# Block-causal attention followed by a bilinear FFN on one core: weight conversions of the first pass emitted step by step, at 0.8 parts a slot, and the first weights loaded ahead of the second pair's q and k

## The chip, the cores and the metric

The kernel runs on one core of a Trainium2 chip. The metric is device time of one launch in microseconds. The engines of the core work in parallel, each through its own instructions in order: PE (TensorE; PEld is its weight load), DVE (VectorE), ACT (ScalarE), POOL (GpSimd), and SP, which here only issues DMAs.

## The reference

Inputs are q, k and v of 8 batches, 8 heads, 576 positions and 64 dimensions in float32, and three weight matrices. Their products are needed to nearly float32 accuracy.

```python
scores = scale * np.matmul(q, k.transpose(0, 1, 3, 2))
mask = block_i >= block_j                 # blocks of 64 positions
scores = np.where(mask, scores, -1000000000.0)
scores = scores - np.max(scores, axis=-1, keepdims=True)
attn = np.exp(scores)
attn = attn / (np.sum(attn, axis=-1, keepdims=True) + 1e-09)
attn_out = np.matmul(attn, v)
x = attn_out.transpose(0, 2, 1, 3).reshape(B * S, H * D)   # 4608 x 512
a = x @ w_a                               # 512 x 1536
b = x @ w_b
return (a * b @ w_out)                    # 1536 x 512
```

## The kernel before

The attention goes through 64 heads in slots, one slot `s` for each head and two more at the end. In slot `s` the list `SLOT` interleaves steps of three generators: `softmax` of head `s` (scores on PE, maxima on DVE, exponentials on ACT, row sums and their reciprocal `rc` on DVE in L442, scaling of the exponentials on POOL in L445), `turn` of the heads one and two slots back (transposes on PE, copies on ACT), and `values` of the head two slots back. The first eight heads (`NATIVE`) multiply in plain float32; from head 8 on q, k, v and the attention are split into a high and a low part, which costs DVE and ACT further instructions (L338, L472, L528 to L532) and SP further DMAs (`spread`, L358 and L359).

From slot 10.2 on (`MOE_FROM`) the first pass of the FFN is woven into the slots: `first_pass` computes a, b, their product and its share of the output for the first four of twelve blocks of w_a, w_b and w_out. `want(now)` says how many of its products are due. The rest of the first pass and the other eight blocks follow when attention is over.

The weights come from the host as 64-bit floats in pairs of 32-bit words and are converted on the chip. For the first pass that is done by `convert_w` in twelve parts: two for each of four blocks of w_a and w_b (`wab0` to `wab3`), then one for each block of w_out (`wo0` to `wo3`). One part is fetched by SP into one of two `raw` buffers (L124, 128x1024 words) one part ahead of its use, and then goes through six DVE instructions in five steps, each step ending at a `yield`: L139 and L143 (integer operations on the raw words), L145, L147, L149, which read what the ones before left, and L113, which subtracts the rounded value and leaves the low part; ACT adds L140 (after L139) and the copy in L110 (after L149). L147 is the last one that reads the raw buffer.

In the slot loop a step of the attention is emitted, then so many conversion steps as are due. Before, they come in whole parts: the number due is five times a whole number, which rises by one at each slot's end.

The written order is not yet the engines' order: a scheduler arranges the instructions of each engine ahead of time, from dependences and priorities. SP's DMAs are issued in its order; one whose buffer is still in use holds up what stands behind it.

Of the kernel before, what the change touches and what calls it, by code (L numbers as in the profile page):

```python
# [20 lines left out]
EPS = 1e-9  # L21
CONV_POOL = 1
CONV_POOL2 = 0
CONV_PER_SLOT = 1.0
CONV0 = 1
HL_DVE = False
MOE_FROM = 10.2
FR = 6
# [24 lines left out]
def attention_then_bilinear_ffn(  # L53
# [10 lines left out]
    nc = tc.nc  # L64
# [5 lines left out]
    wab, wo = wab.bitcast(I32), wo.bitcast(I32)  # L70
# [4 lines left out]
    F1 = 4  # L75
# [17 lines left out]
    def pool(stack, name, bufs, side="left", **kw):  # L93
        return stack.enter_context(tc.tile_pool(name=name, bufs=bufs, side=side, **kw))
# [10 lines left out]
    def f32(ap):  # L105
        return ap.bitcast(F32)

    def split(hi, lo, src, hi_eng, lo_eng):
        if hi_eng is nc.scalar:
            nc.scalar.copy(hi, src)  # L110
        else:
            hi_eng.tensor_copy(hi, src)
        return lo_eng.tensor_tensor(lo, src, f32(hi), op=ALU.subtract)  # L113
# [8 lines left out]
    def fetch(src, nm):  # L122
        raw = wpool.tile([P, 512, 2], I32, tag="raw", name=f"raw{nm}", bufs=2)
        nc.sync.dma_start(raw.rearrange("p n w -> p (n w)"), src)  # L124
        return raw

    def convert(raw, nm, paced):

        hi, mid = raw[:, :, 1], raw.bitcast(U16)[:, :, 1]
        s, m, x = (wpool.tile([P, 512], I32, tag=f"cv_{x}", name=f"{x}{nm}") for x in "smx")  # L130
        sf, mf, xf = (t.bitcast(F32) for t in (s, m, x))
        v = nc.vector

        def step(ins):
            if paced:
                behind_of(ins, "hf")


        step(v.tensor_scalar(s, hi, 20, 0x7FF, op0=ALU.logical_shift_right, op1=ALU.bitwise_and))  # L139
        nc.scalar.activation(s, s, AF.Relu, scale=2.0 ** 23, bias=shift)  # L140
        yield

        step(v.tensor_scalar(m, hi, 0xFFFFF, 0x100000, op0=ALU.bitwise_and, op1=ALU.bitwise_or))  # L143
        yield
        step(v.scalar_tensor_tensor(mf, mid, 2.0 ** -16, m, op0=ALU.mult, op1=ALU.add))  # L145
        yield
        step(v.scalar_tensor_tensor(s, hi, -0x80000000, s, op0=ALU.bitwise_and, op1=ALU.bitwise_or))  # L147
        yield
        step(v.tensor_tensor(xf, mf, sf, op=ALU.mult))  # L149
        return xf, mf  # L150
# [4 lines left out]
    def parts(fs):  # L155
        return [(f, i) for f in fs for i in range(KP)] + [(f, KP) for f in fs]

    def new_wo(f):
        w_sb[f][1] = wopool.tile([P, 2, DO], F32R, tag="wo", name=f"wo{f}")

    def sums(hi, lo, xf, t, paced):

        x, t = (y.rearrange("p (q n) -> p q n", n=P) for y in (xf, t))
        v = nc.vector
        nc.scalar.copy(hi[:, :3], x[:, 1:])
        for d, a, b, op in (
            (0, x[:, 0], x[:, 3], ALU.add),
            (1, t[:, 0], x[:, 1], ALU.subtract),
            (2, x[:, 1], x[:, 0], ALU.subtract),
            (3, x[:, 2], t[:, 1], ALU.subtract),  # L170
        ):
            ins = v.tensor_tensor(t[:, d], a, b, op=op)
        if paced:
            behind_of(ins, "hf")
        nc.scalar.copy(hi[:, 3:], t)
        yield
        v.tensor_tensor(lo[:, :3], x[:, 1:], f32(hi[:, :3]), op=ALU.subtract)
        v.tensor_tensor(lo[:, 3:], t, f32(hi[:, 3:]), op=ALU.subtract)

    def convert_w(todo, lo_eng, paced=False, stage=None):  # L180

        def ahead(f, i):
            return fetch(wab[f, :, i] if i < KP else wo[f], f"w{f}_{i}")

        raw = ahead(*todo[0])
        for k, (f, i) in enumerate(todo):
            now, raw = raw, ahead(*todo[k + 1]) if k + 1 < len(todo) else None
            xf, spare = yield from convert(now, f"w{f}_{i}", paced)
            if stage:
                st = stage.tile([P, 2, NW if i < KP else NO, P], F32R, tag="st", name=f"st{f}_{i}")  # L190
            if i == KP:
                if not stage and w_sb[f][1] is None:
                    new_wo(f)
                o = st.rearrange("p j c n -> p j (c n)") if stage else w_sb[f][1]
                split(o[:, 0], o[:, 1], xf, nc.scalar, lo_eng)
            elif f < F1:
                ab = w_sb[f][0]
                hi, lo = (ab[:, j, i].rearrange("p c n -> p (c n)") for j in range(2))
                split(hi, lo, xf, nc.scalar, lo_eng)
            else:  # L200
                ab = st if stage else w_sb[f][0][:, i]
                yield from sums(ab[:, 0], ab[:, 1], xf, spare, paced)
            if stage:
                f -= F1 + F2
                nc.sync.dma_start(wod[f] if i == KP else wabd[f, i], f32(st).rearrange("p j c n -> p (j c n)"))
            yield

    marks = []
    lo_eng = [nc.gpsimd]
# [101 lines left out]
    def load_pair(p):  # L311

        b, h = divmod(2 * p, H)
        n = f"{b}_{h}"
        if 2 * p < NATIVE:
            qp = apool.tile([P, 1, SQ], F32, tag="q2", name=f"qp{n}", bufs=3)
            kp = apool.tile([P, 2, S], F32, tag="k2", name=f"kp{n}", bufs=3)
        else:
            qp = apool.tile([P, 2, SQ], F32, tag="qp", name=f"qp{n}", bufs=1)
            kp = apool.tile([P, 2, S], F32, tag="kp", name=f"kp{n}", bufs=1)  # L320
        nc.sync.dma_start(kp[:, 1], kT[b, h:h + 2].rearrange("h d s -> (h d) s"))
        nc.sync.dma_start(qp[:, 0], qT[b, h:h + 2].rearrange("h d s -> (h d) s"))
        pairs[p] = qp, kp
        for j in range(2):
            heads[2 * p + j] = {"q": qp[j * D:(j + 1) * D, 0], "k": kp[j * D:(j + 1) * D, 1]}
# [6 lines left out]
    def split_q(p):  # L332
        qp = pairs[p][0]
        if 2 * p < NATIVE:
            nc.vector.tensor_scalar_mul(qp[:, 0], qp[:, 0], SCALE)
            return
        nc.scalar.mul(qp[:, 1].bitcast(F32R), qp[:, 0], SCALE)
        behind_of(nc.vector.scalar_tensor_tensor(  # L338
            qp[:, 0], qp[:, 0], SCALE, qp[:, 1], op0=ALU.mult, op1=ALU.subtract), "rc")
# [234 lines left out]
    LAG = 2  # L574
    per_slot = 2 * F1 * (2 * 3 * NCC + 3 * NO) // H
    behind = 3 * F1 * NO
    conv = convert_w(parts(range(F1)), nc.vector)
    n_moe = n_conv = 0
    for p in range(2):
        load_pair(p)  # L580
        split_q(p)

    def want(now):

# [14 lines left out]
    for s in range(NH + LAG):  # L599
        p, odd = divmod(s + 4, 2)  # L600
        if p < NH // 2 and not odd:
            load_pair(p)
        if s < NH:
            load_v(s)
        steps = []
        for what, i, m in SLOT:
            i += s
            if 0 <= i < NH:
                steps.append((gens.get((what, i)) or gens.setdefault((what, i), what(i)), m))
        due = k = 0  # L610
        for g, m in steps:
            mark = next(g)
            if not m:
                continue
            for _ in range(KEEP.get((s, k), 0)):
                keep = keep or ps_t.tile([P, W], F32, tag="av", name="keep")
                nc.tensor.matmul(keep, z[:, :P], z, start=True, stop=True)
            marks.append(mark)
            if k == 1 and 0 < s <= NH:
                split_v(s - 1)  # L620
            if k == (3 if odd else 4) and s + 2 < NH:
                if not odd and s:
                    split_q((s + 2) // 2)
                    split_k((s + 2) // 2)
            if k == (3 if odd else 6) and s + 2 < NH:
                spread(s + 2)
            k += 1
            due += m
            now = s + due / fill
            while n_conv < 5 * int(now * CONV_PER_SLOT + CONV0):  # L630
                next(conv, None)
                n_conv += 1
            if now > MOE_FROM and moe is None:
                moe = first_pass()
            while moe and n_moe < want(now):
                next(moe)
                n_moe += 1
# [135 lines left out]
    raw = load_x(0)  # L773
    conv = convert_w(parts(range(F1, F1 + F2)), nc.vector, paced=True)
    n_conv = 0
# [15 lines left out]
    stage = pool(left, "stage", 1, reuse_waits="tile")  # L791
# [12 lines left out]
    for ps_ in range(2):  # L804
        fs = list(range(F1 + ps_ * F2, F1 + (ps_ + 1) * F2))
        for tt in range(NT2):
# [21 lines left out]
            todo = [(j, o) for j in (1, 0) for o in range(NO)]  # L828
            hs = {}
            nm = f"z{ps_}_{tt}"  # L830
            for i, f in enumerate(fs):
# [5 lines left out]
                if i == 0 and not lastp:  # L837
                    raw = load_x((tt + 1) % NT2)
# [15 lines left out]
            if ps_ == 0 and tt == 0:  # L854
                background(1e4)
                conv = convert_w(parts(range(F1 + F2, NF)), nc.vector, paced=True, stage=stage)
                n_conv, start, k, pace = 0, 0, 0, STEP2
# [47 lines left out]
```

## Time and profile before

| what | value |
|---|---|
| median of 3 runs | 1249.47 us (1249.38 to 1254.89) |
| profiled execution | 1247.89 us, span of its instructions 1246.1 us |
| granted TensorE clock | 0.999 |
| busy share of the span | PE 98%, PEld 94%, DVE 78%, ACT 57%, POOL 33% |
| reciprocals of heads 0, 7, 10, 14 and 22 (start) | 14.93, 72.66, 105.20, 144.17, 222.48 us |
| conversion of the first pass, from the first L139 to the last L113 | 11.45 to about 103 us |

A name such as `wab<-xw` reads output from input. The reciprocal (L442) occurs once per head, so its times show the pace of the slots: about 8 us a slot up to head 7, then 8 to 13, and pairs of 10.3 and 9.1 us from about head 26.

### The profile page before, as it was taken

To read this page: it belongs to the slowest core of one execution; us is meant where nothing else is said; L and a number is where in the kernel's file an instruction comes from. 1 tells how busy PE (TensorE), PEld (TensorE's weight loads), DVE (VectorE), ACT (ScalarE), POOL (GpSimd) and SP (SyncE) were. 2 spreads that over 40 slices of the span, in tenths; PEclk is the share of its full clock that TensorE was granted. 3 is DMA by queue.
4 is the path that set the end of the run, shared out by engine and by line. 5 is a ranking of instruction groups with operands and counts; after the bars stand their busy time and mean duration, and the time that the engine had idled before them with its cause. 6 is when DMAs were issued, how large, how long until landed. Compare 5 with 4: busy or idle time off the path is not lost.

```text
span 1246.1 us, 23349 instructions
## 1 busy us (share of the span) xinstructions
PE 1219.6 (98%) x7849; PEld 1165.8 (94%) x7849; DVE 976.5 (78%) x2483; ACT 704.4 (57%) x1770; POOL 414.7 (33%) x585
## 2 busy tenths in 40 slices
PE   8988999999999999999999999999999999999998
PEld 5677998999999999999999899999999999999998
DVE  7988887787887877878789989787768677677654
ACT  6887887878788787887746444344334222222210
POOL 3655666556665566655500022021021000000000
PEclk9999999999999999999999999999999999999999
DMA  6575767776667776677234365275378444144131
GB/s 206 168 210 149 194 162 181 188 176 179 169 165 188 175 178 170 164 189 175 70 105 138 104 148 165 76 194 132 97 198 288 136 144 119 47 140 120 34 102 64
DMA packets 86584, 187.14 MB, mean 150 GB/s; under 512 B 11200, under 2 KB 46016, under 8 KB 86464
## 3 DMA queue, kind: packets, MB, share of 16 engines
q1 hardware_dynamic: 74944, 166.76, 47.9%
q0 software_dynamic: 6912, 9.44, 4.7%
q10 hardware_dynamic: 4608, 9.44, 2.1%
q8 instruction: 63, 1.03, 0.3%
q14 instruction: 57, 0.47, 0.1%
HBM read 87.03 MB, written 47.19 MB: 108 GB/s over the span
## 4 chain that ended last, share of the span: by engine, by line
PE 78%; DVE 12%; DMA 4%; ACT 3%; issue 2%; POOL 1%; SPq 0%; ACTq 0%; DVEq 0%; POOLq 0%
PE pso_z L757 14%; PE ps L217 12%; PE psx_z L711 8%; PE psw_z L711 8%; PE psv_z L711 7%; PE tp L468 7%; PE pso L217 5%; PE s L392 4%; PE psy_z L711 4%; PE av L517 3%; PE av L523 3%; PE sl L392 2%; DVE nm L398 1%; DMA kp<-kT 1%; DMA xr<-xd 1%
## 5 line engine op out<-in xcount | busy, mean ns | idle before, releaser
L217 PE MATMUL ps<-xh,wab 128*128 128x288 f32 x1024 | 241.8, 303 | 0.2 <-ACT a L241 0.2
L757 PE MATMUL pso_z<-h_z,wo 128*128 128x384 f32 x1152 | 202.3, 334 | 0.0
L757 PEld LDWEIGHTS pso_z<-h_z,wo 128*128 128x128 f32 x1152 | 199.9, 188 | 0.1
L445 POOL TENSOR_SCALAR e<-e,rc 128x512 f32<-128x512 f32 (+3 forms) x256 | 154.5, 617 | 133.9 <-DVE rc L442 115.7
L217 PEld LDWEIGHTS ps<-xh,wab 128*128 128x128 f32 x1024 | 172.2, 188 | 3.8 <-ACT a L241 0.4
L472 DVE TENSOR_TENSOR al<-tp,ah 128x512 fp32r<-128x512 f32 x224 | 131.5, 608 | 29.8 <-ACT ah L470 29.3
L217 PE MATMUL ps<-xl,wab 128*128 128x288 f32 x512 | 153.8, 300 | 0.0
L110 ACT CAST h_z<-u_z 128x384 fp32r<-128x384 f32 x96 | 49.3, 513 | 172.4 <-DVE u_z L736 160.6
L470 ACT CAST ah<-tp 128x512 fp32r<-128x512 f32 x224 | 116.6, 533 | 51.1 <-PE tp L468 48.2
L468 PE MATMUL tp<-ident,e 128*128 128x128 f32 x832 | 134.3, 275 | 9.0 <-POOL e L445 4.5
L820 POOL DMA_DIRECT2D part<-pt x48 | 42.2, 953 | 292.1 <-ACT pt L819 291.9
L217 PE MATMUL pso<-hh,wo 128*128 128x288 f32 x512 | 125.7, 307 | 1.0 <-ACT hh L110 0.8
L468 PEld LDWEIGHTS tp<-ident,e 128*128 128x128 f32 x832 | 99.4, 140 | 24.1 <-POOL e L445 10.4
L401 ACT ACTIVATE e<-s,nm 128x192 f32<-128x192 f32 (+2 forms) x192 | 101.8, 530 | 32.9 <-DVE nm L398 23.8
L711 PE MATMUL psx_z<-xh,wab 128*128 128x384 f32 x384 | 116.4, 339 | 2.8 <-DVE u_z L729 2.7
L711 PE MATMUL psv_z<-xh,wab 128*128 128x384 f32 x384 | 116.3, 338 | 2.0 <-DVE u_z L738 1.4
L711 PE MATMUL psw_z<-xh,wab 128*128 128x384 f32 x384 | 116.0, 338 | 0.0
L398 DVE TENSOR_REDUCE nm<-s 128x1 f32<-128x128 f32 (+3 forms) x256 | 109.7, 431 | 2.3
L217 PEld LDWEIGHTS ps<-xl,wab 128*128 128x128 f32 x512 | 96.4, 188 | 3.4
L217 PEld LDWEIGHTS pso<-hh,wo 128*128 128x128 f32 x512 | 86.7, 189 | 2.7 <-ACT hh L110 1.4
L392 PE MATMUL s<-k,q 128*128 128x256 f32 x336 | 81.3, 322 | 2.8 <-ACT e_s L401 1.5
L113 POOL TENSOR_TENSOR v<-vr,v 128x320 fp32r<-128x320 f32 x56 | 49.6, 886 | 90.5 <-ACT v L110 64.2
(142 smaller groups left out, 2841.1 us busy)
## 6 DMA issues: line engine op xcount, KB each, us to landing
k<-kp SPq DMA_DIRECT2D x112, 288.0 KB, 3.7
xr<-xd SPq DMA_DIRECT2D x48, 384.0 KB, 4.0
q<-qp SPq DMA_DIRECT2D x112, 160.0 KB, 2.7
raww<-wab SPq DMA_DIRECT2D x24, 512.0 KB, 3.8
qp<-qT SPq DMA_DIRECT2D x32, 320.0 KB, 3.2
vr<-vm SPq DMA_DIRECT2D x64, 160.0 KB, 3.2
kp<-kT SPq DMA_DIRECT2D x32, 288.0 KB, 3.5
xd<-xf ACTq DMA_DIRECT2D x32, 288.0 KB, 3.2
```

Source lines behind the costliest of these rows:

```text
L110: nc.scalar.copy(hi, src)
L113: return lo_eng.tensor_tensor(lo, src, f32(hi), op=ALU.subtract)
L217: mm = nc.tensor.matmul(ps, w_, d_, start=(i == 0), stop=(i == n - 1))
L392: mark = nc.tensor.matmul(ps[:, :w], qm[:, q0[t]:q0[t] + P], kk[:, :w], start=(i == 0), stop=(i == len(ks) - 1))
L398: nc.vector.tensor_reduce(nm[:, t:t + 1], view, axis=AX.X, op=ALU.max, negate=True)
L401: nc.scalar.activation(out, view, AF.Exp, bias=bias, accum_out=sm[:, t, :1])
L445: nc.gpsimd.tensor_scalar(ev, ev, rc[:, t:t + 1], 1.0, op0=ALU.mult, op1=ALU.mult)
L468: mark = nc.tensor.transpose(tp[:, c], src, ident)
L470: nc.scalar.copy(ah[:, :m, cols], tp[:, :m])
L472: return nc.vector.tensor_tensor(al[:, :m, cols], tp[:, :m], f32(ah[:, :m, cols]), op=ALU.subtract)
L711: nc.tensor.matmul(ps, wt[:, i, iw], j[:, ix], start=start and kp == 0 and i == 0 and j is xh, stop=kp == KP - 1 and i == 1, skip_group_ch ...
L757: nc.tensor.matmul(ps, wt[:, a, osl], b, start=i == 0, stop=i == 3 * len(fs) - 1)
```

## The change

The pace of the conversions becomes 0.8 parts a slot, with a lead of 1.2 parts rather than 1, and the number due is rounded to steps, not to whole parts, so that between two attention steps mostly one conversion step or none is emitted. The last one is due at 13.5 slots, before at 11. The fetch of the first part is emitted right after the loads of heads 0 and 1 (pair 0) and handed to `convert_w` as `raw`; before, it was emitted in slot 0, behind the loads of three pairs and of the first v. The second fetch, which `convert_w` emits itself, stays in slot 0.

```diff
-CONV_PER_SLOT = 1.0
-CONV0 = 1
+CONV_PER_SLOT = 0.8
+CONV0 = 1.2
...
-    def convert_w(todo, lo_eng, paced=False, stage=None):
+    def convert_w(todo, lo_eng, paced=False, stage=None, raw=None):
...
-        raw = ahead(*todo[0])
+        raw = raw or ahead(*todo[0])
...
-    conv = convert_w(parts(range(F1)), nc.vector)
     n_moe = n_conv = 0
-    for p in range(2):
-        load_pair(p)
-        split_q(p)
+    load_pair(0)
+    split_q(0)
+    conv = convert_w(parts(range(F1)), nc.vector, raw=fetch(wab[0, :, 0], "w0_0"))
+    load_pair(1)
+    split_q(1)
...
-            while n_conv < 5 * int(now * CONV_PER_SLOT + CONV0):
+            while n_conv < int(5 * (now * CONV_PER_SLOT + CONV0)):
```

What the engines get differs up to about head 14; behind it the orders are the same. In the rows below, the last number of a name counts tiles; ahead of it stand block and part or batch and head (`sw0_2` is of w_out's block 0, `nm0_7` of head 7).

SP at the start, before: three pairs of k and q (`kp`, `qp`), then v of head 0, then two parts of weights.

```order
L321 DMA kp0_0_141<-kT 128x576
L322 DMA qp0_0_140<-qT 128x640
L321 DMA kp0_2_146<-kT 128x576
L322 DMA qp0_2_145<-qT 128x640
L321 DMA kp0_4_151<-kT 128x576
L322 DMA qp0_4_150<-qT 128x640
L330 DMA vr0_0_154<-vm 128x320
L124 DMA raww0_0_171<-wab 128x1024
L124 DMA raww0_1_173<-wab 128x1024
L330 DMA vr0_1_213<-vm 128x320
L330 DMA vr0_2_300<-vm 128x320
L321 DMA kp1_0_515<-kT 128x576
```

And now, from the third row on:

```order
L124 DMA raww0_0_145<-wab 128x1024
L321 DMA kp0_2_148<-kT 128x576
L322 DMA qp0_2_147<-qT 128x640
L321 DMA kp0_4_153<-kT 128x576
L322 DMA qp0_4_152<-qT 128x640
L330 DMA vr0_0_156<-vm 128x320
L124 DMA raww0_1_173<-wab 128x1024
L124 DMA raww1_0_186<-wab 128x1024
L330 DMA vr0_1_221<-vm 128x320
L330 DMA vr0_2_308<-vm 128x320
L321 DMA kp1_0_510<-kT 128x576
```

The first part has moved up by five rows, and the third part (`raww1_0`), which stood behind k and q of heads 8 and 9 (`kp1_0`), now stands ahead of them and of two v.

DVE in head 0's softmax, before: all maxima (`nm0_0`) come ahead of the first conversion.

```order
L398 TENSOR_REDUCE nm0_0_156<-s10_0_160 128x1
L398 TENSOR_REDUCE nm0_0_156<-sl0_0_159 128x1
L335 TENSOR_SCALAR qp0_2_145<-qp0_2_145 128x640
L420 TENSOR_REDUCE nb0_0_158<-nm0_0_156 64x2
L421 TENSOR_REDUCE nb0_0_158<-nm0_0_156 64x2
L430 MEMSET s00_0_186 64x64
L430 MEMSET s20_0_195 64x64
L398 TENSOR_REDUCE nm0_0_156<-s00_0_186 128x1
```

And now:

```order
L398 TENSOR_REDUCE nm0_0_158<-s10_0_162 128x1
L139 TENSOR_SCALAR sw0_0_175<-raww0_0_145 128x512
L398 TENSOR_REDUCE nm0_0_158<-sl0_0_161 128x1
L143 TENSOR_SCALAR mw0_0_176<-raww0_0_145 128x512
L420 TENSOR_REDUCE nb0_0_160<-nm0_0_158 64x2
L421 TENSOR_REDUCE nb0_0_160<-nm0_0_158 64x2
L145 SCALAR_TENSOR_TENSOR mw0_0_176<-raww0_0_145,mw0_0_176 128x512
L335 TENSOR_SCALAR qp0_2_147<-qp0_2_147 128x640
L147 SCALAR_TENSOR_TENSOR sw0_0_175<-raww0_0_145,sw0_0_175 128x512
```

The first part's conversion has moved in between head 0's maxima, and it reads the weights (`raww0_0`) ahead of the second pair's q (`qp0_2`).

DVE up to head 7's reciprocal, before:

```order
L147 SCALAR_TENSOR_TENSOR sw0_2_928<-raww0_2_816,sw0_2_928 128x512
L149 TENSOR_TENSOR xw0_2_930<-mw0_2_929,sw0_2_928 128x512
L430 MEMSET s10_7_835 64x64
L139 TENSOR_SCALAR sw1_2_1035<-raww1_2_926 128x512
L398 TENSOR_REDUCE nm0_7_831<-s10_7_835 128x1
L143 TENSOR_SCALAR mw1_2_1036<-raww1_2_926 128x512
L113 TENSOR_TENSOR wo0_79<-xw0_2_930,wo0_79 128x512
L435 TENSOR_REDUCE rc0_7_832<-sm1_123 128x5
L145 SCALAR_TENSOR_TENSOR mw1_2_1036<-raww1_2_926,mw1_2_1036 128x512
L439 TENSOR_REDUCE rc0_7_832<-sm1_123 64x2
L413 MEMSET s11_0_949 64x64
L442 RECIPROCAL rc0_7_832<-rc0_7_832 128x5
```

And now:

```order
L398 TENSOR_REDUCE nm0_7_815<-s20_7_895 128x1
L113 TENSOR_TENSOR wab3_84<-xw3_1_873,wab3_84 128x512
L139 TENSOR_SCALAR sw0_2_1010<-raww0_2_869 128x512
L430 MEMSET s10_7_819 64x64
L143 TENSOR_SCALAR mw0_2_1011<-raww0_2_869 128x512
L398 TENSOR_REDUCE nm0_7_815<-s10_7_819 128x1
L145 SCALAR_TENSOR_TENSOR mw0_2_1011<-raww0_2_869,mw0_2_1011 128x512
L435 TENSOR_REDUCE rc0_7_816<-sm1_123 128x5
L439 TENSOR_REDUCE rc0_7_816<-sm1_123 64x2
L442 RECIPROCAL rc0_7_816<-rc0_7_816 128x5
```

At head 7's reciprocal the conversion stands six instructions further back: in w_out's block 0 (`wo0`) where it stood in block 1.

## Prediction

> **What bounds the kernel now.** I read the page's busy shares and slices first, to see where TensorE has gaps; then busy times over stretches that I cut at the reciprocals of the softmax (L442, one per head); then the groups of DVE and ACT instructions in the part that has conversions; then the chain of waits there, and the timeline of the start.
>
> ```profile
> PE 1219.6 (98%) x7849; PEld 1165.8 (94%) x7849; DVE 976.5 (78%) x2483; ACT 704.4 (57%) x1770; POOL 414.7 (33%) x585
> ...
> PEld 5677998999999999999999899999999999999998
> DVE  7988887787887877878789989787768677677654
> ```
>
> Each digit is a slice of 31 us. From the fifth slice on the weight loads are busy nine tenths and more; in the first four they are at 5 to 7, and DVE at 7 to 9. The second view is busy time per stretch: bounds, length, then busy time (and count) of PE, PEld, DVE, ACT, POOL, then clock, DMA share, GB/s.
>
> ```profile
> 6.36:14.93 8.57, 8.57 (x32) 4.53 (x31) 7.90 (x26) 3.89 (x12) 0.00 (x0) 1.00 0.88 330
> 14.93:31.36 16.43, 14.54 (x84) 8.62 (x80) 15.45 (x44) 14.09 (x38) 10.21 (x11) 1.00 0.42 140
> 31.36:47.55 16.19, 15.34 (x108) 10.66 (x108) 15.67 (x45) 12.99 (x38) 8.74 (x12) 1.00 0.50 141
> 47.55:63.45 15.90, 14.94 (x108) 10.66 (x108) 14.40 (x46) 12.77 (x37) 10.02 (x12) 1.00 0.69 200
> 63.45:72.66 9.21, 8.45 (x61) 5.91 (x58) 8.76 (x26) 8.43 (x23) 5.11 (x6) 1.00 0.61 203
> 72.66:85.50 12.84, 11.26 (x89) 9.25 (x90) 9.68 (x29) 11.37 (x32) 5.97 (x9) 1.00 0.63 160
> 85.50:93.60 8.10, 7.02 (x51) 5.94 (x50) 6.76 (x22) 6.44 (x19) 4.92 (x7) 1.00 0.93 295
> 93.60:105.20 11.60, 10.30 (x65) 8.61 (x64) 11.28 (x32) 8.74 (x25) 6.45 (x8) 1.00 0.52 119
> 105.20:115.07 9.87, 8.20 (x55) 6.86 (x53) 7.30 (x25) 6.57 (x20) 4.97 (x9) 1.00 0.75 198
> 115.07:134.09 19.02, 18.54 (x131) 17.51 (x131) 16.21 (x50) 15.93 (x47) 12.91 (x19) 1.00 0.66 172
> 134.09:144.17 10.08, 9.36 (x66) 8.62 (x65) 8.54 (x25) 8.00 (x23) 6.31 (x8) 1.00 0.56 130
> 144.17:222.48 78.31, 75.95 (x546) 72.28 (x545) 62.71 (x197) 62.40 (x176) 47.97 (x68) 1.00 0.72 184
> 222.48:1246.10 1023.62, 1012.20 (x6462) 992.66 (x6460) 790.86 (x1926) 531.25 (x1294) 289.77 (x403) 1.00 0.53 143
> ```
>
> After 222 us TensorE is busy 1012 of 1024 us: it is the bound, and its work there is not touched. The order of all engines is the same again from about head 14 on, whose reciprocal ends the row at 144.17. So the change is decided in the first 144 us, and what it gains or loses there is carried to the end one for one. In those rows DVE is busy 92 to 97% of 6.36 to 47.55, 95% of the row to 72.66 and 97% of the row to 105.20; in the other rows it has idle time of 1.5, 3.2, 1.3, 2.6 and 2.8 us. TensorE's granted clock is 1.00 throughout.
>
> **What one conversion costs.** Between 11 and 104 us, the groups of DVE (busy us, mean ns) and of ACT that belong to the twelve parts:
>
> ```profile
> L149 DVE TENSOR_TENSOR xw<-mw,sw 128x512 f32<-128x512 f32 x12 | 10.3, 858 | 0.1
> L145 DVE SCALAR_TENSOR_TENSOR mw<-raww,mw 128x512 f32<-128x512 uint16 x12 | 9.2, 766 | 0.1
> L147 DVE SCALAR_TENSOR_TENSOR sw<-raww,sw 128x512 int32<-128x512 int32 x12 | 8.7, 723 | 1.1 <-ACT sw L140 1.1
> L113 DVE TENSOR_TENSOR wab<-xw,wab 128x512 fp32r<-128x512 f32 x8 | 6.5, 814 | 0.0
> L139 DVE TENSOR_SCALAR sw<-raww 128x512 int32<-128x512 int32 x12 | 5.3, 445 | 0.1
> L143 DVE TENSOR_SCALAR mw<-raww 128x512 int32<-128x512 int32 x12 | 5.0, 420 | 0.1
> L113 DVE TENSOR_TENSOR wo<-xw,wo 128x512 fp32r<-128x512 f32 x4 | 2.8, 688 | 0.2 <-ACT wo L110 0.2
> L140 ACT ACTIVATE sw<-sw,shift 128x512 int32<-128x512 int32 x12 | 8.7, 726 | 0.5 <-DVE sw L139 0.4
> L110 ACT CAST wab<-xw 128x512 fp32r<-128x512 f32 x8 | 5.0, 623 | 2.0 <-DVE xw L149 2.0
> ```
>
> DVE: 10.3+9.2+8.7+6.5+5.3+5.0+2.8 = 47.8 us for 72 instructions, 0.66 us each, six to a part. ACT adds 0.73+0.62 = 1.35 us a part. The change adds and removes none of them; it moves them. I counted them between the same reciprocals in the two orders. Before, in the rows of the table from the first: 5, 16, 14, 13, 9, 6, 5, 4, 0, 0. After: 8, 13, 12, 14, 4, 10, 6, 1, 2, 2. So the pacing shows little in what the engines get: at most six instructions (4 us) are later than before, at the row that ends at 72.66, and four are pushed past 105.20, into rows where DVE has idle time.
>
> **The sum, row by row.** Where DVE is the bound, an instruction taken out is worth up to 0.66 us; where it has idle time, one put in costs between nothing and 0.66 us. I take a third of it there: the idle time of those rows (11.4 us) is more than the ten instructions put in (6.6 us), but DVE works in order, so an instruction fills a gap only if it stands ahead of the one that waits.
>
> - To 31.36: three in, three out: 0. Bounds: -1.65 (the idle time of the two rows) and +2.0 (the three are not given back).
> - To 47.55: two out, 1.3 us by DVE. The chain of waits there is ACT and PE for long pieces (below), so half: -0.65; bounds -1.3 and 0.
> - To 63.45: one in: +0.2; bounds 0 and 0.66.
> - To 72.66: five out, 3.3 us by DVE. ACT is busy 8.43 of the 9.21 us; without one relu and one cast it has 7.1, so the row can't fall below that: -2.1; bounds -3.3 and 0.
> - To 85.50: four in, 2.6 us, in 3.16 us of idle time: +0.9; bounds 0 and 2.6.
> - To 93.60: one in: +0.2; bounds 0 and 0.66.
> - To 105.20: three out, 2.0 us; PE is busy 10.30 of 11.60, which leaves 1.3: -1.3; bounds -2.0 and 0.
> - To 115.07, and to 134.09: two in each: +0.45 each; bounds 0 and 1.3 each. The last conversion (wo3) ends right behind head 12's reciprocal, at about 125 us in the old time; the first product that needs it comes later.
>
> Together -0.65+0.2-2.1+0.9+0.2-1.3+0.45+0.45 = -1.85 us. The gains alone make -8.3, the costs alone +8.5.
>
> ```profile
> 38.12 0.65 ACT xh L110 x2
> 38.77 0.97 ACT ah L470 x2
> 39.74 0.40 ACT sw L140
> ...
> 42.56 1.35 PE av L507 x12
> 43.91 0.59 PE tp L468 x4
> 44.50 1.48 PE av L507 x16
> ```
>
> **The load ahead, and what stands behind it on SP.** The rows of the start (DVE, and ACT's two; start, length), and what all DMA engines moved in each us from 0:
>
> ```profile
> 4.77 0.49 DVE L335 TENSOR_SCALAR qp<-qp 128x640 f32<-128x640 f32 x1 [3.37 <-DMA qp<-qT]
> ...
> 6.71 0.29 DVE L398 TENSOR_REDUCE nm<-s 128x1 f32<-128x128 f32 x1
> 7.18 0.69 DVE L398 TENSOR_REDUCE nm<-sl 128x1 f32<-128x512 f32 x1 [0.18 <-PE sl L392]
> ...
> 8.19 0.14 DVE L420 TENSOR_REDUCE nb<-nm 64x2 f32<-64x2 f32 x1
> ...
> 14.93 0.19 DVE L442 RECIPROCAL rc<-rc 128x5 f32<-128x5 f32 x1
> 14.94 0.67 ACT L344 CAST kp<-kp 128x576 fp32r<-128x576 f32 x1
> ...
> 16.36 0.37 ACT L401 ACTIVATE e_s<-s,nb 128x128 f32<-128x128 f32 x1
> ```
>
> ```profile
> GB/s 0 37 271 353 274 235 375 378 352 340 410 385 416 207 86 258 180 0 0 25 286 385 352 98 8 16 20 279 237 152 0 0 0 20 238 238 156 170 204 157
> ```
>
> The first k and q (128x576 and 128x640 floats) are 623 kB; summing the row they are through at 3.9 us, and DVE has them at 4.77, 0.9 later. With the 524 kB of weights (128x1024 ints) third in the queue these land at about 6.8 us, and the next k and q (623 kB) at 8.5. DVE now wants the weights behind the maximum at 6.71, at 7.0, and the second q after L139, the maximum of 0.69, L143, two instructions of 0.14 and L145, 2.6 us more: 9.6. Both are there, with 0.2 and 1.1 us to spare; so I put the load at 0. If the weights took 2 us longer, the first softmax would wait for them: bounds 0 and +2.0, the same that the first row has.
>
> The third part's load now stands on SP ahead of v of heads 1 and 2 and of k and q of heads 8 and 9, and must wait for the first part's L147 to free its buffer, at about 10.8 us (9.6, the q's scaling of 0.49, and L147). Up to and with that k, 1147 kB (524, two times 164, 295) take 3.3 us at some 350 GB/s, and 0.9 to land: 15.0 us. ACT's L344 reads it and ran at 14.94; behind it stands head 1's first exponential, which ran at 16.36. Up to 1.3 us late costs nothing; beyond that each us on SP is one on ACT.
>
> **Rivals.**
> *It does nothing.* The scheduler has reordered the steps so that the counts differ little; PE and ACT set the rows where I see a gain. 1249.5. For it: the chain at 38 to 46 us has no conversion but one relu. Against: DVE at 95 and 97% in the two rows with gains.
> *More collisions of DVE with POOL.* L149 takes 858 ns on average against 688 for L113 into wo of the same shape; by that the conversions lose (858-688)x12+(766-688)x12+(723-688)x12+(814-688)x8 = 4.4 us to stretching.
>
> ```profile
> L445 POOL TENSOR_SCALAR e<-e,rc 128x512 f32<-128x512 f32 (+3 forms) x256 | 154.5, 617 | 133.9 <-DVE rc L442 115.7
> ```
>
> POOL is busy 51 of the 90 us from 14.93 to 105.20. If each of the 48 instructions with two inputs met it by chance, it would wait half of 617 ns in 57% of cases, 8.4 us, 4.0 more than now; with the -1.85 that is +2.1, 1251.6: slower than before. It decides from 1.9 us of added stretching. The Trainium skill, "SBUF — State Buffer", section "SBUF: two separate sides", says that DVE instructions with two inputs in SBUF and GpSimd's hold one port pair in turn, each for the whole instruction. The trace agrees in kind: the two-input groups are stretched, L139 (445 ns) and L143 (420 ns) hardly differ. By the rule with chance meetings the time would be 1251.6, by the measured 4.4 us kept as they are 1247.6; the trace shows half of the rule's 8.4 us now, and I stay with the row.
> *Latency, not throughput.* What is put in lies on the path in full (0.66+2.6+0.66+1.3+1.3 = +6.6) and what is taken out gains nothing, as PE and ACT bind there: 1256. For it: TensorE has little idle time in the row to 105.20. Against: DVE's 11.4 us of idle time where they are put.
> *The whole of DVE's share.* 1.3+3.3+2.0 = -6.6 with nothing paid: 1242.9. For it: DVE idles where they go. Against: ACT's 8.43 us in the row to 72.66.
>
> **How the numbers follow.** The profiled execution took 1247.89 us, 1.6 under the median of the runs (1249.47); it would become 1246.0, and the median 1247.6. Chances: as forecast, -4.5 to -0.5, 0.45; nothing, 0.22; collisions, 0.13; all of DVE's share, 0.13; latency, 0.07. About 0.5% (6.2 us) is what a measurement of this kernel tells from no change; only the last two go beyond it: faster 0.13, same 0.80, slower 0.07. The range leaves out most of the latency case and the outer half of the largest gain: 1242.0 to 1253.0.
>
> **What would show it.** Right: reciprocal of head 7 at about 70 to 72 us rather than 72.66, that of head 10 two us ahead of 105.20, and the same lead at 222. The first reciprocal should come at 15 to 16 us, with the weights' L139 running at about 7.0 and no wait on their DMA. Wrong: a DVE wait for the weights or for the second q before 10 us; ACT's L344 waiting for kp near 15 us; L149 and L145 with means above 0.9 us; the row after head 7 longer by over 2 us; or a time beyond head 14 that does not keep the lead.

## The result, and the profile after

The changed kernel takes 1261.26 us (median of 14 runs, 1255.61 to 1265.43); the kernel before, run beside it, 1252.3 us (14 runs, 1249.03 to 1261.76). The ratio is 1.0071, 95% interval 1.0051 to 1.0091: slower by 0.7%, 9 us, where 2 us of gain were forecast.

The profiled execution took 1255.61 us (span 1253.8), the fastest of the 14. Its page: busy shares, then slices of 31 us of PE and of the granted TensorE clock.

```profile
PE 1222.7 (98%) x7849; PEld 1169.5 (93%) x7849; DVE 974.8 (78%) x2483; ACT 704.0 (56%) x1770; POOL 415.9 (33%) x585
...
PE   8988999999999999999999999999999999999998
...
PEclk9999999999999999999999999999999999999999
```

Nothing stands out here: the mean clock is 0.996 against 0.999 before. The loss shows when the span is cut at the reciprocals, as in the prediction (bounds, length, busy time and count of PE, PEld, DVE, ACT, POOL, then clock, DMA share, GB/s):

```profile
15.70:33.63 17.93, 15.39 (x84) 9.36 (x80) 14.13 (x45) 13.57 (x36) 8.89 (x11) 0.90 0.40 131
33.63:47.83 14.20, 13.48 (x82) 9.20 (x81) 13.75 (x40) 11.51 (x34) 9.52 (x12) 0.88 0.56 161
47.83:67.53 19.70, 19.70 (x141) 14.42 (x140) 16.45 (x48) 15.46 (x42) 8.63 (x12) 1.00 0.63 166
67.53:74.21 6.68, 5.90 (x45) 4.12 (x44) 4.69 (x18) 5.84 (x18) 5.54 (x6) 1.00 0.38 123
74.21:91.82 17.61, 12.49 (x89) 10.47 (x88) 12.55 (x35) 11.88 (x33) 7.74 (x9) 0.90 0.67 171
91.82:103.19 11.37, 9.65 (x71) 8.30 (x69) 8.47 (x24) 8.69 (x26) 6.98 (x8) 1.00 0.74 231
103.19:112.27 9.08, 7.87 (x52) 6.97 (x53) 8.27 (x27) 6.75 (x18) 5.01 (x7) 1.00 0.85 186
...
228.04:1253.80 1025.76, 1012.51 (x6462) 992.57 (x6460) 791.03 (x1926) 530.99 (x1294) 289.23 (x403) 1.00 0.53 143
```

Against before, the rows up to heads 2, 4, 6 and 7 are 1.5 longer, 2.0 shorter, 3.8 longer and 2.5 us shorter; those to heads 8, 9 and 10 are 4.8 and 3.3 longer and 2.5 shorter. At head 14 the changed kernel is 5.3 us behind, at head 22 (228.04 for 222.48) 5.6. New are the clocks of 0.90, 0.88 and 0.90: three stretches of 3.41 us ran at 0.50. Rows of the same columns, cut on that raster of 3.41 us, each half-clock stretch with what comes ahead of it:

```profile
13.81:17.22 3.41, 2.56 (x10) 0.94 (x9) 3.17 (x11) 1.29 (x4) 1.14 (x2) 1.00 0.86 301
17.22:20.64 3.42, 2.25 (x13) 1.28 (x12) 2.14 (x8) 3.42 (x10) 3.42 (x5) 1.00 0.48 151
20.64:24.05 3.41, 2.94 (x10) 1.03 (x9) 2.99 (x11) 2.51 (x8) 0.62 (x1) 1.00 0.59 190
24.05:27.46 3.41, 3.36 (x16) 2.71 (x16) 3.29 (x10) 2.87 (x10) 2.53 (x3) 0.50 0.20 68
...
41.12:44.53 3.41, 2.78 (x12) 1.32 (x13) 3.28 (x10) 2.47 (x11) 3.41 (x5) 1.00 0.66 216
44.53:47.94 3.41, 3.41 (x16) 2.75 (x15) 3.35 (x11) 2.67 (x7) 1.52 (x3) 0.50 0.33 101
...
78.66:82.08 3.42, 0.20 (x2) 0.00 (x0) 2.18 (x6) 0.49 (x2) 1.74 (x3) 1.00 0.89 256
82.08:85.49 3.41, 3.03 (x13) 2.66 (x14) 1.26 (x3) 3.24 (x12) 0.87 (x1) 0.50 0.35 124
```

Ahead of each, TensorE had been less than fully busy; the clock then halves for the next piece, although that piece is full of work. What half the clock does is seen on one group of twelve products. The prediction's chain of before has it at 1.35 us; in the timeline of after, inside the first half-clock stretch and then for the next head, outside of it:

```profile
25.33 2.44 PE L507 MATMUL av<-ah,vr 128*64 128x64 f32 x12
...
34.19 1.37 PE L507 MATMUL av<-ah,vr 128*64 128x64 f32 x12
```

Two waits are new as well (timeline; the bracket is idle time ahead and what ended it):

```profile
17.14 0.67 ACT L344 CAST kp<-kp 128x576 fp32r<-128x576 f32 x1 [2.12 <-DMA kp<-kT]
...
18.24 0.37 ACT L401 ACTIVATE e_s<-s,nb 128x128 f32<-128x128 f32 x1
...
75.95 1.43 SPq L330 DMA_DIRECT2D vr<-vm  x1
...
81.59 0.46 ACT L110 CAST v<-vr 128x320 fp32r<-128x320 f32 x1 [4.20 <-DMA vr<-vm]
...
82.46 0.90 PE L392 MATMUL s<-k,q 128*128 128x320 f32 x2 [3.60 <-ACT e_s L401]
```

The first: k of heads 8 and 9 lands at 17.1 us, ACT waits for it, and head 1's first exponential comes 1.9 us later than before (16.36). The second: SP issues the raw v of head 8 only at 75.95, and in ACT's new order its cast stands ahead of head 8's exponentials, so these, and PE behind them, wait 3.6 us. DVE's groups (lines with conversions, up to 125 us) answer for the collisions:

```profile
L149 DVE TENSOR_TENSOR xw<-mw,sw 128x512 f32<-128x512 f32 x11 | 9.0, 817 | 0.2
L147 DVE SCALAR_TENSOR_TENSOR sw<-raww,sw 128x512 int32<-128x512 int32 x12 | 8.8, 731 | 1.3 <-ACT sw L140 1.2
L145 DVE SCALAR_TENSOR_TENSOR mw<-raww,mw 128x512 f32<-128x512 uint16 x12 | 8.6, 716 | 0.1
...
L143 DVE TENSOR_SCALAR mw<-raww 128x512 int32<-128x512 int32 x12 | 6.2, 516 | 0.1
...
L139 DVE TENSOR_SCALAR sw<-raww 128x512 int32<-128x512 int32 x12 | 6.1, 505 | 2.2 <-DMA raww<-wo 2.1
L113 DVE TENSOR_TENSOR wab<-xw,wab 128x512 fp32r<-128x512 f32 x8 | 5.6, 699 | 0.1
```

L149, L145 and L113 became shorter (858, 766 and 814 ns before), L139 and L143 longer (445 and 420).

### The profile page after: what moved, and what is told of

Same layout as the page of the kernel before. It is cut to its first block, busy times and chain, and to the rows that moved or that the text cites. A ratio compares the mean times of both kernels' runs of the same rounds, so it can differ in the third digit from the quotient of the medians.

```text
span 1253.8 us, 23351 instructions
## 1 busy us (share of the span) xinstructions
PE 1222.7 (98%) x7849; PEld 1169.5 (93%) x7849; DVE 974.8 (78%) x2483; ACT 704.0 (56%) x1770; POOL 415.9 (33%) x585
## 4 chain that ended last, share of the span: by engine, by line
PE 76%; DVE 11%; DMA 6%; ACT 4%; issue 2%; POOL 1%; SPq 1%; ACTq 0%; DVEq 0%; POOLq 0%
PE pso_z L758 14%; PE ps L217 11%; PE psx_z L712 8%; PE psw_z L712 8%; PE psv_z L712 7%; PE tp L468 6%; PE pso L217 4%; PE s L392 4%; PE psy_z L712 4%; PE av L517 3%; PE av L523 3%; PE sl L392 2%; DMA q<-qp 2%; DMA kp<-kT 1%; PE av L507 1%
## 5 line engine op out<-in xcount | busy, mean ns | idle before, releaser
L401 ACT ACTIVATE e<-s,nm 128x448 f32<-128x448 f32 (+2 forms) x192 | 101.6, 529 | 30.2 <-DVE nm L398 21.2
L113 POOL TENSOR_TENSOR v<-vr,v 128x320 fp32r<-128x320 f32 x56 | 49.4, 882 | 92.7 <-ACT v L110 70.5
```

The lines of the kernel that those rows point to most:

```text
L401: nc.scalar.activation(out, view, AF.Exp, bias=bias, accum_out=sm[:, t, :1])
```

## The experiments

The 13 other runs of the changed kernel had a mean clock of 0.987 to 0.992, so the profiled one shows the least of it. Time at half clock, worked out as 2 x (1 - clock) x span, is 25.4 us on average for the changed kernel. 114 runs of the kernel before, in e1 and beside the experiments, average 6.9 us; over them, time = 1249.39 + 0.37 x (us at half clock), correlation 0.83. By that line, an estimate from the scatter of one kernel, 18.5 us more at half clock cost 6.8 us of the 9.0.

Theory B takes this for the cause: TensorE does too little in some pieces of the first 90 us, the clock halves, and that is most of the loss. Theory A, the rival, says that new waits (the order of loads and casts) are the cause and the clock a by-product. The instrument is a list that the kernel has already: `KEEP` puts idle products on zeros (L617, 128x512, result unused) into the first slots, 4 in the first and 12 in the second.

All kernels that were run stand in the table ("over the line" is the median less the line's value at the kernel's own mean half-clock time). Two single runs far off, 1965 us in e4 and 1318 us in e10, are not in the means of the clock. One run of the kernel before is not in the line: it shows a clock of 0.946 and took 1254.0 us, where the line would give 1299, and nothing on record says why.

| kernel | median us | mean clock | ratio to before, 95% | over the line |
|---|---|---|---|---|
| the change | 1261.3 | 0.990 | 1.0071 (1.0051 to 1.0091) | 2.5 |
| e1 before | 1251.9 | 0.996 | 1.0007 (0.9982 to 1.0032) | -0.9 |
| e2 pacing alone | 1259.7 | 0.990 | 1.0077 (1.0059 to 1.0094) | 1.2 |
| e3 load ahead alone | 1260.9 | 0.990 | 1.0083 (1.0059 to 1.0108) | 2.1 |
| e4 change, four v | 1257.9 | 0.995 | 1.0042 (1.0021 to 1.0062) | 4.0 |
| e5 before, 12 products fewer | 1259.1 | 0.990 | 1.006 (1.004 to 1.008) | 0.4 |
| e6 change, 14 more | 1257.5 | 0.996 | 1.0051 (1.0031 to 1.0072) | 4.1 |
| e7 change, 64 in the heads | 1260.1 | 0.998 | 1.0068 (1.0041 to 1.0094) | 9.2 |
| e8 before, 64 in the heads | 1262.4 | 0.998 | 1.0087 (1.0056 to 1.0117) | 10.7 |
| e9 change, four v, 14 more | 1255.2 | 0.997 | 1.0026 (1.0005 to 1.0047) | 3.1 |
| e10 before, 14 more | 1249.3 | 0.999 | 0.9977 (0.9957 to 0.9997) | -1.3 |
| e11 load ahead, 14 more | 1249.6 | 0.999 | 0.9984 (0.9968 to 1.0000) | -0.7 |
| e12 pacing, 14 more | 1255.8 | 0.996 | 1.0022 (1.0002 to 1.0042) | 2.3 |
| e13 e9 and 12 in the heads | 1255.4 | 0.997 | 1.0032 (1.0011 to 1.0052) | 3.2 |
| e14 e12 and 12 in the heads | 1254.2 | 0.998 | 1.001 (0.999 to 1.003) | 2.7 |
| e15 e11 and 12 in the heads | 1256.0 | 0.997 | 1.0026 (1.0005 to 1.0048) | 3.9 |

**e1: the kernel before, for its clocks.** No edit.

> The kernel before, unchanged, for the granted clock of its runs. Theory A (load order: in the changed kernel v of head 8 is loaded behind k and q spreads on SP, and ACT waits 4.2 us for it ahead of head 8's exponentials): median near 1252, nothing more. Theory B (TensorE's clock falls to half for 3.4 us at a time after pieces in which it does little, more often in the changed kernel): the runs differ in clock, the fast ones near 0.999 and 1249, the slow ones near 0.99 and 1256 or more; per 0.001 of clock some 0.7 us. If all runs show 0.998 or more whatever their time, B falls as an explanation of the medians.

1251.9 us; its runs at a clock of 0.999 and more took 1247.5 to 1250.0, one at 0.990 took 1257.6. The kernel before has the loss in some runs already. The clock isn't all of it: the slowest, 1262.0 us, had 0.995.

**e2: the pacing alone.**

```diff
-CONV_PER_SLOT = 1.0
-CONV0 = 1
+CONV_PER_SLOT = 0.8
+CONV0 = 1.2
...
-            while n_conv < 5 * int(now * CONV_PER_SLOT + CONV0):
+            while n_conv < int(5 * (now * CONV_PER_SLOT + CONV0)):
```

> The new pacing alone; the first fetch as before. Its SP and ACT orders have head 8's v where the changed kernel has it. Theory A: as slow as the changed kernel, 1259 to 1262, ratio 1.005 to 1.009, with ACT's wait for v of 3 to 5 us near 78 us. Rival C (the fetch ahead of the second pair's q and k does it): 1250 to 1253, ratio 0.998 to 1.002. Theory B: as slow as the changed kernel, clock near 0.99.

**e3: the load ahead alone.**

```diff
-    for p in range(2):
-        load_pair(p)
-        split_q(p)
+    load_pair(0)
+    split_q(0)
+    conv = convert_w(parts(range(F1)), nc.vector, raw=fetch(wab[0, :, 0], "w0_0"))
+    load_pair(1)
+    split_q(1)
```

> The fetch ahead alone, with the old pacing in whole parts. Theory A: its order has head 8's v where the kernel before has it, so 1251 to 1253, ratio 0.999 to 1.001. Rival C: 1258 or more, ratio 1.005 or more. Theory B: goes with the clock, near the one before.

1259.7 and 1260.9 us: each half of the change costs what the whole does, so the loss is no sum of separate waits. In e3, head 8's v is loaded and cast where it was before, and the loss is there all the same. In e2 the wait for v is there, 2.85 us (87.73). Both kernels have the mean clock of the whole change, 0.990. In e2 a piece with next to no TensorE work stands right ahead of 20.48 us at half clock (rows as above):

```profile
15.18:18.59 3.41, 0.11 (x1) 0.00 (x0) 3.34 (x8) 2.55 (x7) 3.04 (x2) 1.00 0.31 100
18.59:22.00 3.41, 2.91 (x8) 1.50 (x9) 1.21 (x3) 1.52 (x4) 2.74 (x5) 0.50 0.45 154
```

In e3 the first half-clock stretch comes earlier still:

```profile
8.82:12.23 3.41, 2.64 (x9) 1.09 (x8) 3.29 (x10) 1.85 (x5) 0.00 (x0) 1.00 0.90 352
12.23:15.64 3.41, 3.41 (x9) 2.30 (x8) 2.60 (x7) 2.27 (x7) 0.00 (x0) 0.50 0.70 185
```

**e4: the change with a fourth buffer for the raw v**, so that its load need not wait.

```diff
-        vr = heads[i]["vr"] = apool.tile([P, NCH + 1, D], F32, tag="vr", name=f"vr{b}_{h}", bufs=3)
+        vr = heads[i]["vr"] = apool.tile([P, NCH + 1, D], F32, tag="vr", name=f"vr{b}_{h}", bufs=4)
```

> The changed kernel with four buffers for v instead of three: v of head 8 is then ordered ahead of the k and q spreads on SP, and its cast behind head 8's exponentials on ACT. Theory A: the wait of 4.2 us goes and most of the loss with it: 1253 to 1256, ratio 1.000 to 1.003, one window of half clock fewer. Theory B: the clock stays near 0.99 since the pieces at 20 and 41 us are as before: 1258 to 1260, ratio 1.004 to 1.007.

1257.9 us; the cast moves behind the exponentials, and the step from head 7 to head 8 falls from 17.6 to 13.7 us (12.8 before). The median is 3.4 us lower and lies between the ranges of the two theories. How much of that is the wait for v can't be told from it: the mean clock rises from 0.990 to 0.995, which by the line is worth more than the whole gain, and the fourth buffer changes SP's and ACT's orders in many other places, from 12 us on.

**e5: the kernel before with 12 idle products fewer.** The order of ACT, DVE, POOL and SP is the same row for row.

```diff
-KEEP = {(0,3):4,(1,0):2,(1,1):2,(1,2):2,(1,3):6}
+KEEP = {(0,3):4}
```

> The kernel before without the 12 idle products that it feeds to TensorE in the second slot (the four of the first slot stay); the order of all other work is as before, and the products' results are used by nothing. Theory B (the loss comes from stretches of 3.4 us in which TensorE's clock is halved because it did too little before): TensorE does less near 10 to 15 us, so more half-clock stretches, mean clock 0.993 or lower, 1256 to 1262 us, ratio 1.003 to 1.008. Rival (the loss comes from what waits for what, and the clock is a by-product): nothing waits for these products, 1250 to 1252, ratio 0.998 to 1.000.

1259.1 us, ratio 1.006 (1.004 to 1.008), 8.7 us more than the kernel before beside it: nearly the whole loss of the change, without the change, by taking away products whose results nobody reads. The page's clock, and the pieces around 17 us:

```profile
PEclk7999999999999999999999999999999999999999
```

```profile
13.60:17.02 3.42, 0.21 (x1) 0.00 (x0) 3.20 (x12) 1.92 (x4) 1.15 (x1) 1.00 0.50 170
17.02:20.43 3.41, 3.31 (x11) 2.51 (x12) 2.76 (x6) 2.91 (x9) 3.41 (x5) 0.50 0.01 5
20.43:23.84 3.41, 3.41 (x10) 1.57 (x8) 1.96 (x5) 2.62 (x7) 1.52 (x2) 0.50 0.67 229
```

This is theory B's case: less work for TensorE, 9 us more time. It falls 0.4 us from the line.

**e6: the change with 14 idle products more**, in the rest of the second slot and in the third. POOL and SP keep their order, DVE and ACT but for a few rows.

```diff
-KEEP = {(0,3):4,(1,0):2,(1,1):2,(1,2):2,(1,3):6}
+KEEP = {(0,3):4,(1,0):2,(1,1):2,(1,2):2,(1,3):6,(1,4):2,(1,5):2,(1,6):2,(2,0):2,(2,1):2,(2,2):2,(2,3):2}
```

> The changed kernel with 14 idle products more (128x512, results unused) between about 14 and 20 us. Theory B: the half-clock stretches near 20 to 30 us go, mean clock 0.994 to 0.999, 1252 to 1256 us, ratio to before 1.001 to 1.004. Rival: the products only cost, 14 times about 0.2 us where TensorE is late: 1261 to 1264.

1257.5 us, 3.8 less than the change alone, with nearly the same order. The pieces that the changed kernel has at 2.56, 2.25 and 2.94 us of PE are now full, and the half-clock stretch behind them is gone:

```profile
13.81:17.22 3.41, 3.41 (x12) 1.67 (x12) 3.17 (x12) 1.34 (x3) 0.66 (x1) 1.00 0.95 301
17.22:20.64 3.42, 3.42 (x16) 1.69 (x14) 2.51 (x7) 2.69 (x9) 3.42 (x6) 1.00 0.45 162
20.64:24.05 3.41, 3.41 (x13) 1.87 (x12) 3.31 (x8) 2.30 (x7) 1.14 (x1) 1.00 0.61 202
24.05:27.46 3.41, 3.41 (x20) 1.97 (x20) 3.14 (x13) 2.32 (x7) 1.76 (x2) 1.00 0.04 13
```

At head 7 it stands at 73.0 us (74.2 without the products, 72.7 before). But the wait for head 8's v is still there and still halves the clock, at 81.75 us: the step to head 8 takes 18.3 us. The median lies 1.5 us above the range expected.

**e7 and e8: the change, and the kernel before, with two idle products ahead of each group of transposes of the first eight heads**, 64 in all.

```diff
             tp = ps_t.tile([P, 4, P], F32, tag="tp", name=f"tp{n}_{t}", bufs=2)
+            if native:
+                for _ in range(2):
+                    nc.tensor.matmul(tp.rearrange("p c n -> p (c n)"), z[:, :P], z, start=True, stop=True)
```

> The changed kernel with two idle products (128x512) ahead of each group of transposes of the eight heads of the first pass, 64 in all, into the tile that the transposes then overwrite. Theory B: hardly a half-clock stretch in the first 90 us, mean clock 0.998 or more, 1251 to 1255 us. Rival: 64 products more, up to 13 us of TensorE, 1261 to 1270.

> Control: the same 64 idle products in the kernel before. Theory B: the few half-clock stretches that it has go as well, mean clock about 0.999, 1248 to 1251 us, ratio 0.997 to 0.9995. Rival: they cost what they take, 1253 to 1260. The difference between this and the changed kernel with the same products is what the order and the waits alone cost, by theory B 2 to 4 us.

1260.1 and 1262.4 us. As remedies both failed: the products cost what they take, some 10 us. As a pair they show no difference (their intervals overlap), with the clock at 0.998 in both and no half-clock stretch between 6 and 1250 us in either profile; head 14 comes at 153.2 and 153.0 us. That does not settle what the order costs. The products shifted the scheduler's order in both, and the wait for head 8's v now stands in both profiles: 2.51 us in e7 (93.31), 2.60 in e8 (93.23), where the kernel before has none.

**e9: the change with both remedies** (the edits of e4 and e6).

> The changed kernel with both remedies: a fourth buffer for the raw v, and the 14 idle products more between 14 and 20 us. Theory (clock, and the late v of head 8 that makes TensorE idle near 80 us): mean clock 0.997 or more, 1250 to 1254 us, ratio to before 1.000 to 1.003; head 7 to head 8 takes about 13 us rather than 17.6. Rival (the pacing itself loses time by its order): no better than with the products alone, 1256 to 1259.

1255.2 us, ratio 1.0026 (1.0005 to 1.0047): about two thirds of the loss are gone, not all; the median lies above the range of the theory. Head 8 now takes 15.0 us (93.4 less 78.4), not the 13 expected.

This profile shows something that the mean clock leaves out. Its views give the clock as 1.00 from the start, but the trace's first clock record comes only at 17.9 us, and ahead of it TensorE runs at about half speed. Nine of the idle products, in e6 and then in e9:

```profile
10.93 2.33 PE L618 MATMUL keep<-z 128*128 128x512 f32 x9
```

```profile
14.16 4.04 PE L618 MATMUL keep<-z 128*128 128x512 f32 x9
```

In 15 of the 17 profiles the first record comes at 4.4 to 7.1 us, in e9 at 17.9 and in e12 at 14.3; there the first reciprocal comes at 19.93 and 20.28 us, elsewhere at 14.9 to 17.5. At 0.37 us for each us at half clock, the 11 or 8 us more come to some 4 or 3 us, an estimate, that neither the mean clocks nor the line count. How many of the runs without a profile began so is not on record.

**e10 and e11: the kernel before, and the load ahead alone, with the 14 products of e6.**

> Control: the kernel before with the same 14 idle products. Theory: clock 0.998 or more in all runs, 1248 to 1251 us, ratio 0.998 to 1.000, since they lie where TensorE has idle time. Rival: each costs its 0.2 us, 1252 to 1254, and then the same 2 to 3 us are to be taken off the changed kernel with them.

> The load ahead alone, old pacing, with the 14 idle products. Theory: the half-clock stretches near 20 to 40 us go, clock 0.995 or more, 1250 to 1255 us, against 1260.9 without them. Rival (the load ahead loses time by what waits for it): 1258 to 1262, whatever the clock.

1249.3 us, ratio 0.9977 (0.9957 to 0.9997), and 1249.6 us, ratio 0.9984 (0.9968 to 1.0000). For the load ahead nothing of the loss is left: 1260.9 us without the products, 1249.6 with them, and TensorE does more work for it. It is no clean cut, as the products also shift the order of ACT and DVE from 22 us on and SP's from 45 us on, and in e10 the order of the same engines; the clean cuts are e5, e6 and e12, in which the other engines keep their order but for a few rows. e10 beats both kernels of this case, by 2.9 us against the one before (0.4 to 5.4 by the interval).

**e12: the pacing alone with the 14 products.**

> The new pacing alone, old place of the first load, with the 14 idle products. Theory: clock 0.995 or more, 1250 to 1255 us, against 1259.7 without them. Rival (the pacing loses time by its order): 1258 to 1262, whatever the clock.

1255.8 us, against 1259.7 without them: a part came back, by products alone, as SP, DVE and POOL have the same order in both and ACT all but the same. It lies 0.8 us above the range expected. Its profile still has two half-clock stretches of 6.83 us, from 24.6 and 75.8 us. The second begins within a wait of PE for head 7's exponentials (timeline), which ACT ran behind a cast of k and one of weights:

```profile
76.04 1.43 PE L392 MATMUL s<-kp,qp 64*128 64x320 f32 x2 [1.26 <-ACT e_s L401]
```

**e13, e14, e15: what is left of the pacing's loss.** Four idle products ahead of the value products of heads 5, 6 and 7, in e9, e12 and, as a control, e11.

```diff
             an, vr = ah, t["vr"]
+            for _ in range(4 if i in (5, 6, 7) else 0):
+                nc.tensor.matmul(av, z[:, :P], z, start=True, stop=True)
```

> The changed kernel with the fourth v buffer, the 14 idle products, and 12 more: four ahead of the value products of heads 5, 6 and 7, where TensorE waits for the exponentials of the next head (near 64, 73 and 82 us). Theory (what is left of the pacing's loss is the half-clock stretch near 76 us): mean clock 0.999 or more, 1249 to 1252 us, ratio 0.998 to 1.001. Rival (what is left is the order of the pacing itself): still 1254 to 1257, whatever the clock.

> The new pacing alone with the 14 idle products and the 12 ahead of the value products of heads 5, 6 and 7. Theory: mean clock 0.998 or more, 1249 to 1252 us, against 1255.8 without the 12. Rival: 1254 to 1257, whatever the clock.

> Control for the cost of the 12 products where nothing is to be repaired: the load ahead alone with the 14 idle products and these 12. 1249.6 without them; they take 0 to 2.5 us, so 1249 to 1252, clock 0.999.

1255.4, 1254.2 and 1256.0 us. The first two gained nothing that can be told apart from none; the control lost 6.3 us. It is no clean control: the products shifted the scheduler's order in it (head 8's v now stands behind a `spread` of q on SP, and some of DVE's conversions moved), and its clock fell from 0.999 to 0.997. In e13 and e14 the half-clock stretch near 76 us is gone from the profile, and the time did not fall, as the rival of e13 and e14 had it. The order of ACT and DVE shifts in them too, from 73 and 75 us on.

What is left of the pacing's loss, 2 to 4 us over the line in e4, e6, e9, e12, e13 and e14, stays open. The late start is not all of it, as the profiles of e13 and e14 start like the others and took 1253.8 and 1254.0 us at a clock of 0.999. The wait for k at 17 us is not needed for it, as e12 and e14 do not have it. Nor does all of it lie where the order changed: of the 5.9 and 6.1 us by which the spans of e13 and e14 exceed that of the profile before, 2.0 and 3.2 had come by the last head's reciprocal, and the rest came behind it, where one half-clock stretch lies near 881 us.

## Why the prediction was wrong, step by step

- *TensorE's granted clock is 1.00 throughout.* This is the step that failed. It was read off before's profile and taken over to after without a rival. The kernel before keeps its clock only because idle products fill its second slot; e5 takes 12 of them and loses 9 us. Both halves of the change shift when TensorE has work between 9 and 25 us, and from there the clock falls: at a mean clock of 0.990 rather than 0.997 this is 6.8 of the 9.0 us by the line, and putting 14 idle products into those pieces took back 3.8 us of the change (e6) and 3.9 of the pacing alone (e12). The Trainium skill, "TensorE: Matmul & The Clock Gate", section "Why this matters for your kernels", asks for no gap of over about 3 us between bursts of products. The trace agrees at 78.66 us and in e2 and e5, where PE had gaps of 3.60, 3.80 and 3.31 us; at 24.05 and 44.53 us the clock halved behind pieces with PE busy 2.94 and 2.78 of 3.41 us, so the rule does not catch these.
- *Load ahead: the weights cost no wait.* Right: L139 ran at 7.45 us with no wait on a DMA (7.0 forecast), the second q was used at 9.74 (9.6), and the first reciprocal came at 15.70 (15 to 16).
- *Load ahead: k of heads 8 and 9 lands at 15.0, and up to 1.3 us late is free.* Missed by 2.1 us: at 17.1, and ACT waited 2.12 us. SP issued that load at 12.18 us, where before it went at 7.46, and from 10.8 to 17.1 us the DMA engines moved 236 GB/s, not the 350 that I took. The 1.3 us were misread too: the cast itself stands ahead of that exponential, and the two begin 1.10 us apart (17.14 and 18.24), which leaves 0.3 us from 15.0 to 16.36. The named sign of failure, L344 waiting near 15 us, came.
- *The gains, row by row.* Right in place and sign, too small in size: the row to head 7 fell by 2.5 us (2.1 forecast), to head 10 by 2.5 (1.3), to head 4 by 2.0 (0.65). The gain to head 10 is no proof of its reason: e10, with the old pacing and the 14 products, gains 2.4 us there as well.
- *The costs, row by row.* Wrong where DVE had idle time: 3.8 us for 0.2 to head 6, 4.8 for 0.9 to head 8, 3.3 for 0.2 to head 9. The first is TensorE at 100% with 141 products in place of 108; in e6, with no half-clock stretch ahead of it, the row still has 123 and takes 18.13 us, so part of it is work that moved in from the row before. The second is head 8's v and the half-clock piece behind it; the third is not explained. I counted only DVE's instructions there, not what SP's and ACT's order would make of a load between them.
- *Collisions of DVE with POOL (+4.0).* Did not come: the two-input groups became shorter, and the six groups shown, 45.0 us before, are 44.3 now with one L149 (0.8 us) fewer, about the same.
- *Latency (1256, chance 0.07).* The nearest number, and the wrong mechanism: its 6.6 us were DVE instructions on the path, and with the clock repaired no such loss is left for the load ahead (e11); for the pacing the table leaves 2 to 4 us, whose cause is open.
- *What is gained or lost by head 14 is carried to the end.* Right to head 22 (5.3, then 5.6 us), and 7.9 at the last head; the 2.3 us between are not explained.
- *From the fifth slice on the weight loads are busy nine tenths and more.* Misread for the seventh slice, the 23rd and the last, which have an 8; nothing in the sum rests on it.

## What to carry to other kernels

Before costing instructions that move, ask what the move does to TensorE's clock: cut the first microseconds into pieces of 3.4 us, see which are short of work, and put "the clock halves here" among the rivals, with its price. Which of the short pieces will trigger it could not be told here from their busy share. Where a kernel carries idle work to hold the clock, its place is tuned to the old order, and a change of order has to move it along. Look at the clock of many runs and not of the one profile: 0.996 in the profile stood for 0.987 to 0.992 in the rest. And compare the first products of a profile with those of another, since a slow start shows there and not in the mean clock.

## What the runs showed of the hardware

- The clock halves for whole pieces of 3.41 us (or several on end: 13.65 us in e5, 20.48 in e2). The raster does not start with the program: two profiles of the same kernel, before and e1, have the first clock record at 5.47 and 6.62 us. One kernel's runs differ with the clock: 1247.5 us at 0.999, 1257.6 at 0.990 (e1).
- Half clock can outlast the weak piece: in e2 it went on to 39.07 us with PE busy all of each piece from 22.0 us on, and in e9 from the start to 17.9 us with PE busy without a gap from 3.8.
- A microsecond at half clock went with 0.37 us of the whole on average, not with the half that TensorE would lose as the bound. That some of it falls into time in which TensorE waits anyway is likely and not shown.
- A half-clock stretch can follow a piece in which PE was busy 86% of the time by the trace (20.64 us), and others with 66% (17.22 us) had none behind them. What decides between them these runs don't show.
